# First transform stage of an FFT convolution: one 121-column product, or two column tiles of 64 and 57

## The chip, the cores and the metric

The kernel runs on one core of one Trainium2 chip. The metric is the device time of one execution in microseconds. The kernel before takes 2770.51 us, the median of 2 runs (2769.9 to 2771.11).

## What is computed

The reference chains three things. First a long convolution with a gate: with `u = x * v` of shape (2, 12480, 128) and a filter made by a small two-layer network, `y = irfft(rfft(u) * rfft(h))` along the sequence, and the result is `x * y`. Then two pairs of dense layers follow on the 24960 tokens: `(g @ w_out)` with `h = tokens @ w_in`, once with `g = h * cos(h)` and once with `g = h * clip(h + 3, 0, 6) / 6`, width 128 to 2048 to 128.

```python
Uf = np.fft.rfft(u, n=L, axis=1)
Hf = np.fft.rfft(h_filt, n=L, axis=0)
y = np.fft.irfft(Uf * Hf[None, :, :], n=L, axis=1)[:, :S, :]
return (x * y)
```

The change touches the convolution alone.

## The kernel before, in words

The convolution is done as a two-dimensional transform: a series of 111 x 113 points (N1 x N2) is transformed along the 111 first, then along the 113. It runs in 64 iterations (`for i in range(NG)`), each on two of the 128 channels, with the stages of several iterations interleaved by hand: the program is written in the order in which each engine is to run it, and every engine works through its own queue in that order.

The names that matter are these.

- `uf` (made on DVE, line 225) and `hf` (made on POOL, line 237) hold, for each series, 57 columns of sums at columns 0 to 56 and 57 columns of differences at columns 64 to 120 (OD = 64, KE = 121). Columns 57 to 63 are zero.
- `f1` is the constant table of the transform along 111 points: 56 cosines and 56 negative sines in 112 columns (K1 = 56).
- `s1(i, g)` is the first transform stage, three times per iteration: g = 2 for the filter, g = 0 and 1 for the two batch entries. It makes four products (line 252). Each has 121 columns of `uf` or `hf` as the stationary operand and the 112 columns of `f1` as the moving operand, and puts 121 partitions x 112 values into the PSUM tile `ap`. The operands are float32, and the trace shows each such product as two passes, a weight load and a matmul each, so four products are eight passes.
- ACT then copies `ap` to the SBUF tile `at`, in two instructions: partitions 0 to 63 with the cosine half first (line 254), and partitions 64 to 120 with the two halves exchanged (line 255).
- `s2h` and `s2u` (line 364) are the second stage, on `at`: PSUM tiles `xh` and `xp`. `s2i` (line 408, PSUM tile `bp`) and `s1i` (line 422, PSUM tile `v`) transform back. DVE and POOL do the element-wise work between them; `fin` on POOL (lines 450 to 464) finishes a result, and `make_q` and `make_hf` on POOL (lines 204 to 237) prepare the next input. Two `decoder` generators unpack the weights of the dense layers in the same loop, on DVE, ACT and POOL.

On TensorE's queue an iteration reads: four products of `s1` for the filter, four of `s2i`, four of `s1`, four of `s2i`, four of `s1`, then `s2h`, `s2u` and `s1i`. The dense layers come after the loop and make up most of the time.

Of the kernel before, what the change touches and what calls it, by code (L numbers as in the profile page):

```python
# [9 lines left out]
FP32 = mybir.dt.float32  # L10
# [13 lines left out]
N1, N2 = 111, 113  # L24
N = N1 * N2
NP1 = 112
K1 = 56
M2 = 57
MP = 2 * M2
OD = 64  # L30
KE = OD + M2
# [12 lines left out]
def kernel(  # L44
# [19 lines left out]
    nc = tc.nc  # L64
# [84 lines left out]
    def conv_phase(cctx):  # L149
        const = cctx.enter_context(tc.tile_pool(name="const", bufs=1))  # L150
# [8 lines left out]
            k = sum(d >= o for o in HS[1:])  # L159
            return h_p[k][:, d - HS[k]:d - HS[k] + n, :]  # L160

        f1 = const.tile([N1, 2 * K1], FP32, name="f1")
        f2 = const.tile([N2, MP], FP32, name="f2")
        sig = const.tile([NP1, MP], FP32, name="sig")
        cs = const.tile([KE, 2, N2], FP32, name="cs")
# [2 lines left out]
        uf = [const.tile([N1, B, 2, CH, 128], FP32, name=f"uf{k}") for k in range(2)]  # L168
        hf = [const.tile([N1, 2, CH, 128], FP32, name=f"hf{k}") for k in range(2)]
# [72 lines left out]
        def s1(i, g, pool=None):  # L242
            if i >= NG:
                return
            if i not in a_t:
                a_t[i] = p_2.tile([KE, 2, 12, K1], FP32, tag="at", name="at")
            at = a_t[i]
            ap = (pool or ps_a).tile([KE, 4, 2, K1], FP32, tag="a", name="ap")
            for q in range(4):
                s, c = divmod(q, CH)  # L250
                st = (uf[i % 2][:, g, s, c] if g < 2 else hf[i % 2][:, s, c])[:, :KE]
                nc.tensor.matmul(out=ap[:, q].rearrange("p z k -> p (z k)"), lhsT=st, rhs=f1)  # L252
            src = ap.rearrange("p q z k -> p z q k")
            nc.scalar.copy(at[:OD, :, 4 * g:4 * g + 4, :], src[:OD])
            nc.scalar.copy(at[OD:, ::-1, 4 * g:4 * g + 4, :], src[OD:])

        with ExitStack() as hctx:
            hp = hctx.enter_context(tc.tile_pool(name="hp", bufs=1))
# [69 lines left out]
            for k in range(len(chunks)):  # L328
                if k + 8 < len(chunks):
                    load_pos(k + 8)  # L330
                if k + 1 < len(chunks):
                    mlp(k + 1)
                filt(k)
                if k == len(chunks) - 3:
                    make_p(0, ps_r)
                    make_u(0)
                if k >= len(chunks) - 2:
                    s1(0, k - len(chunks) + 2)
                if k == 3:
                    nc.sync.dma_start(out=sig, in_=c_sig)  # L340
                    load(0)
                    nc.sync.dma_start(out=f1, in_=c_f1)
                    nc.sync.dma_start(out=cs, in_=c_cs)
                if k == 5:
                    make_q(0)
                    load(1)
                    nc.sync.dma_start(out=f2, in_=c_f2)
                    nc.sync.dma_start(out=gm, in_=c_g)
                if k == 7:
                    make_q(1)  # L350
                if k == 9:
                    load(2)
# [121 lines left out]

        make_hf(0)
        s1(0, 2)
        make_p(1)
        make_u(1)
        make_hf(1)
        for i in range(NG):  # L480
            load(i + 3)
            store(i - 4)
            s1(i + 1, 2)
            s2i(i - 2, 0)
            s1(i + 1, 0, ps_c)
            s2i(i - 2, 1)
            s1(i + 1, 1)
            make_p(i + 2)
            make_q(i + 2)
            make_hf(i + 2)  # L490
            s2h(i)
            if i >= 3:
                mk_w(i - 3)
            step_decode()
            make_u(i + 2)
            if i >= 3:
                fin(i - 3)
            s2u(i)
            if i >= 2:
                s1i(i - 2)  # L500
            mk_pq(i)
            mk_y(i)
# [236 lines left out]
    with tc.manual_schedule():  # L739
        nc.gpsimd.memset(b_exp, 1150.0)  # L740
        nc.gpsimd.memset(b_max, 254.0 * 2.0 ** 23)
        nc.gpsimd.memset(b_one, 1.0)
        with ExitStack() as cctx:
            conv_phase(cctx)
        with ExitStack() as mctx:
            moe_phase(mctx)


def _order():
    ord2 = np.concatenate([np.arange(1, M2), [0], N2 - np.arange(1, M2)])  # L750
    return ord2, (N2 * np.arange(N1)[:, None] + N1 * ord2[None, :]) % N
# [15 lines left out]
def _constants():  # L767
    ord2, idx = _order()
    n1 = np.arange(N1)
    f32 = np.float32  # L770
    k1 = np.arange(K1)
    th1 = 2 * np.pi * ((n1[:, None] * k1[None, :]) % N1) / N1
    f1 = np.concatenate([np.cos(th1), -np.sin(th1)], axis=1)
    k2 = np.arange(N2)
    thi = 2 * np.pi * ((k2[:, None] * ord2[None, :M2]) % N2) / N2
    f2 = np.concatenate([np.cos(thi), np.sin(thi)], axis=1)
    cs = np.zeros((KE, 2, N2))
    cs[:M2, 0] = cs[:M2, 1] = np.cos(thi.T)
    cs[OD:, 0], cs[OD:, 1] = np.sin(thi.T), -np.sin(thi.T)
    wt = (np.where(k1 == 0, 1.0, 2.0) * 0.5 / N)[:, None]  # L780
    co, si = np.cos(th1.T) * wt, np.sin(th1.T) * wt
    g = np.zeros((2 * K1, 2, NP1))
    g[:K1, 0, :N1], g[K1:, 0, :N1] = co, -si
    g[:K1, 1, :N1], g[K1:, 1, :N1] = -si, -co
    win = np.zeros((N1, MP))
    win[:, :N2] = np.where(idx < S, np.exp(f32(-0.01) * idx.astype(f32)), 0.0)
    sig = np.zeros((NP1, MP))
    sig[:N1, :N2] = 1.0 - 2.0 * (idx % 2)
    return idx, [a.astype(f32) for a in (f1, cs, f2, g, win, sig)]
# [53 lines left out]
```

## Time and profile before

| What | Value |
|---|---|
| median of the runs | 2770.51 us (2769.9 to 2771.11) |
| the profiled execution's own time | 2773.05 us |
| its span | 2771.3 us |
| loop of the convolution | about 40 to 553 us of the span |
| dense layers | from about 572 us to the end |
| TensorE busy over the span | 2740.0 us (99%) |
| granted TensorE clock, mean | 0.995 of 2.4 GHz |

An engine's busy time is the union of its instructions' times. The end of a matmul is modelled, and one matmul's record overlaps the next one's; what a pass costs in a stream is therefore the distance from one start to the next and not the recorded duration. Weight loads (PEld) run beside the matmuls (PE).

### The profile page before, as it was taken

What the parts mean: (1) busy time and instruction counts of PE and PEld (TensorE: products, weight loads), DVE (VectorE), ACT (ScalarE), POOL (GpSimd) and SP (SyncE); (2) the same over time, 40 slices, a digit from 0 to 9 for tenths busy, and PEclk for the clock granted to TensorE, in tenths of its full rate; (3) what the DMA queues carried; (4) which work ended last, traced back from release to release, by engine and by line L of the source; (5) the groups of instructions that cost most, each with busy time, mean ns of one, the idle gap of its engine ahead of it and who ended that gap; (6) DMA issues with size and microseconds to landing.
All of it is one profiled execution on the core that took longest, in us unless ns stands there. A gap on an engine that the chain in (4) does not pass through costs nothing.

```text
span 2771.3 us, 39495 instructions
## 1 busy us (share of the span) xinstructions
PE 2740.0 (99%) x12941; PEld 2205.5 (80%) x12941; DVE 2348.6 (85%) x3182; ACT 2268.1 (82%) x3287; POOL 2448.3 (88%) x1551
## 2 busy tenths in 40 slices
PE   8999999979999999999999999999999999999999
PEld 7777777768888888888888888888888888888888
DVE  6888888778888888888888888888888888888887
ACT  4777777778888888888888888888888888888885
POOL 5899999878989888889888898988889888889897
PEclk9999999989999999999999999999999999999999
DMA  3333333210000000000000000000000000000000
GB/s 113 87 95 96 94 96 87 72 31 8 16 9 16 8 16 8 16 8 16 12 13 16 8 16 8 16 8 16 8 16 16 8 16 8 16 8 16 8 8 12
DMA packets 88289, 79.50 MB, mean 29 GB/s; under 512 B 57139, under 2 KB 78870, under 8 KB 88086
## 3 DMA queue, kind: packets, MB, share of 16 engines
q1 hardware_dynamic: 87798, 76.77, 10.0%
q8 instruction: 106, 1.74, 0.3%
q14 instruction: 97, 0.79, 0.1%
q10 hardware_dynamic: 288, 0.20, 0.0%
HBM read 51.19 MB, written 25.74 MB: 28 GB/s over the span
## 4 chain that ended last, share of the span: by engine, by line
PE 88%; POOL 9%; ACT 1%; DVE 1%; issue 1%; DMA 0%; POOLq 0%; SPq 0%; ACTq 0%; DVEq 0%
PE acc L676 39%; PE hb L610 20%; PE ha L610 19%; PE ap L252 3%; PE bp L408 2%; PE xp L364 2%; PE v L422 2%; POOL z L464 2%; POOL hf L237 1%; POOL z L463 1%; POOL z L450 1%; POOL q L204 1%; PE xh L364 1%; POOL q L207 1%; POOL hm L232 1%
## 5 line engine op out<-in xcount | busy, mean ns | idle before, releaser
L666 POOL TENSOR_TENSOR lo<-g,hi 128x1024 fp32r<-128x1024 f32 (+1 forms) x390 | 939.4, 2409 | 239.9 <-PE ha L610 160.6
L641 POOL TENSOR_TENSOR lo<-g,hi 128x1024 fp32r<-128x1024 f32 (+1 forms) x392 | 941.9, 2403 | 8.4 <-ACT hi L638 7.8
L620 ACT ACTIVATE k<-ha,biasq 128x512 int32<-128x512 f32 (+1 forms) x768 | 507.8, 688 | 310.2 <-PE ha L610 305.8
L631 DVE TENSOR_TENSOR g<-ha,r 128x512 f32<-128x512 f32 (+1 forms) x768 | 500.0, 690 | 286.3 <-ACT r L630 286.2
L610 PE MATMUL ha<-xh,wi 128*128 128x512 f32 (+1 forms) x1536 | 546.1, 396 | 10.5 <-ACT xh L587 7.4
L610 PE MATMUL hb<-x2h,vi 128*128 128x512 f32 (+1 forms) x1564 | 554.7, 395 | 0.3 <-DVE g L631 0.3
L630 ACT ACTIVATE r<-r,biaspi 128x512 f32<-128x512 f32 (+1 forms) x776 | 520.6, 720 | 0.2
L621 DVE SCALAR_TENSOR_TENSOR r<-k,ha 128x512 f32<-128x512 int32 (+1 forms) x768 | 489.8, 679 | 4.0 <-ACT k L620 3.5
L649 DVE SCALAR_TENSOR_TENSOR g<-q,hb 128x1024 f32<-128x1024 f32 (+1 forms) x391 | 473.1, 1210 | 8.8 <-ACT q L648 8.8
L663 DVE SCALAR_TENSOR_TENSOR hi<-q,hb 128x1024 fp32r<-128x1024 f32 (+1 forms) x390 | 470.4, 1206 | 0.0
L648 ACT ACTIVATE q<-hb,bias 128x1024 f32<-128x1024 f32 (+1 forms) x391 | 434.6, 1111 | 21.8 <-PE hb L610 17.9
L676 PE MATMUL acc<-hi,wo 128*128 128x512 f32 (+1 forms) x1568 | 429.4, 396 | 0.0
L676 PE MATMUL acc<-hi,vo 128*128 128x512 f32 (+1 forms) x1568 | 427.6, 395 | 0.0
L638 ACT CAST hi<-g 128x1024 fp32r<-128x1024 f32 (+1 forms) x388 | 403.0, 1039 | 0.0
L610 PEld LDWEIGHTS ha<-xh,wi 128*128 128x128 f32 x1536 | 289.9, 189 | 78.8 <-issue 11.5
L676 PEld LDWEIGHTS acc<-hi,wo 128*128 128x128 f32 x1568 | 295.8, 189 | 69.2
L610 PEld LDWEIGHTS hb<-x2h,vi 128*128 128x128 f32 x1564 | 294.6, 188 | 70.0 <-ACT k L620 0.7
L676 PEld LDWEIGHTS acc<-hi,vo 128*128 128x128 f32 x1568 | 294.6, 188 | 65.9
L610 PE MATMUL hb<-x2l,vi 128*128 128x512 f32 (+1 forms) x782 | 308.1, 394 | 0.0
L610 PE MATMUL ha<-xl,wi 128*128 128x512 f32 (+1 forms) x768 | 303.2, 395 | 0.0
L676 PE MATMUL acc<-lo,wo 128*128 128x512 f32 (+1 forms) x784 | 246.5, 396 | 0.0
L676 PE MATMUL acc<-lo,vo 128*128 128x512 f32 (+1 forms) x784 | 245.8, 394 | 0.0
(116 smaller groups left out, 3408.2 us busy)
## 6 DMA issues: line engine op xcount, KB each, us to landing
x<-in_x_dram SPq DMA_DIRECT2D x64, 199.5 KB
v<-in_v_dram SPq DMA_DIRECT2D x64, 199.5 KB
scr<-z SPq DMA_DIRECT2D x128, 98.9 KB
out_dram<-o SPq DMA_DIRECT2D x47, 256.0 KB
xf<-scr SPq DMA_DIRECT2D x17, 256.0 KB
wst<-in_wi_dram SPq DMA_DIRECT2D x8, 512.0 KB
wst<-in_wo_dram SPq DMA_DIRECT2D x8, 512.0 KB
pt<-in_post_dram SPq DMA_DIRECT2D x14, 224.0 KB
```

The lines of the kernel that those rows point to most:

```text
L610: nc.tensor.matmul(out=hs[c][:, 0, :n], lhsT=w["i", e][:, sl], rhs=r[:, :n], start=(k == 0), stop=(k == 2))
L620: nc.scalar.activation(out=k[:, c, :n], in_=h, func=ACTF.Identity, bias=biasq, scale=1.0 / TWO_PI)
L621: nc.vector.scalar_tensor_tensor(out=un.r[:, c, :n], in0=k[:, c, :n], scalar=-TWO_PI, in1=h, op0=ALU.mult, op1=ALU.add)
L630: nc.scalar.activation(out=rc, in_=rc, func=ACTF.Sin, bias=biaspi, scale=1.0)
L631: nc.vector.tensor_tensor(out=un.g[:, c, :n], in0=h, in1=rc, op=ALU.mult)
L638: nc.scalar.copy(un.hi[:, :, :n], un.g[:, :, :n])
L641: nc.gpsimd.tensor_tensor(out=un.lo[:, :, :n], in0=un.g[:, :, :n], in1=un.hi[:, :, :n], op=ALU.subtract)
L648: nc.scalar.activation(out=un.r[:, c, :n], in_=h, func=ACTF.Relu, bias=bias3, scale=1.0)
L649: nc.vector.scalar_tensor_tensor(out=un.g[:, c, :n], in0=un.r[:, c, :n], scalar=6.0, in1=h, op0=ALU.min, op1=ALU.mult)
L663: nc.vector.scalar_tensor_tensor(out=un.hi[:, c, :n], in0=un.r[:, c, :n], scalar=6.0, in1=h, op0=ALU.min, op1=ALU.mult)
L666: nc.gpsimd.tensor_tensor(out=un.lo[:, :, :n], in0=un.g[:, :, :n], in1=un.hi[:, :, :n], op=ALU.subtract)
L676: nc.tensor.matmul(out=acc[e][:, :n], lhsT=w["o", e][:, sl], rhs=r[:, c, :n], start=(u == 0 and c == 0 and k == 0), stop=(u == KFF // 2 - ...
```

## The change

The four products of `s1` are made in two pieces each. One takes the 64 columns of the sums and writes PSUM partitions 0 to 63; the other takes the 57 columns of the differences and writes PSUM partitions 64 to 120. In the compiled program the first has a tile of 128 rows x 64 columns of the array at column 0, the second one of the same size at column 64; every other product of the kernel has the whole 128 x 128 array. The table `f1` gets a third block, the cosines again, so that the second piece can use columns 56 to 167 (negative sines first, then cosines): the halves come out exchanged already, and one ACT instruction copies all 121 partitions.

```diff
-        f1 = const.tile([N1, 2 * K1], FP32, name="f1")
+        f1 = const.tile([N1, 3 * K1], FP32, name="f1")
...
-                st = (uf[i % 2][:, g, s, c] if g < 2 else hf[i % 2][:, s, c])[:, :KE]
-                nc.tensor.matmul(out=ap[:, q].rearrange("p z k -> p (z k)"), lhsT=st, rhs=f1)
-            src = ap.rearrange("p q z k -> p z q k")
-            nc.scalar.copy(at[:OD, :, 4 * g:4 * g + 4, :], src[:OD])
-            nc.scalar.copy(at[OD:, ::-1, 4 * g:4 * g + 4, :], src[OD:])
+                st = uf[i % 2][:, g, s, c] if g < 2 else hf[i % 2][:, s, c]
+                o = ap[:, q].rearrange("p z k -> p (z k)")
+                nc.tensor.matmul(out=o[:OD], lhsT=st[:, :OD], rhs=f1[:, :2 * K1])
+                nc.tensor.matmul(out=o[OD:], lhsT=st[:, OD:KE], rhs=f1[:, K1:])
+            nc.scalar.copy(at[:, :, 4 * g:4 * g + 4, :], ap.rearrange("p q z k -> p z q k"))
...
-    f1 = np.concatenate([np.cos(th1), -np.sin(th1)], axis=1)
+    f1 = np.concatenate([np.cos(th1), -np.sin(th1), np.cos(th1)], axis=1)
```

TensorE's queue for one iteration of the loop reads as follows in the kernel before (x4: four instructions of that form; L252 is `s1`, L408 is `s2i`, L364 is `s2h` and `s2u`, L422 is `s1i`):

```order
L252 MATMUL ap<-f_79,hf_86 121x112 x4
L408 MATMUL bp<-f_80,y 112x114 x4
L252 MATMUL ap<-f_79,uf_84 121x112 x4
L408 MATMUL bp<-f_80,y 112x114 x4
L252 MATMUL ap<-f_79,uf_84 121x112 x4
L364 MATMUL xh<-at,cs 113x224 x2
L364 MATMUL xp<-at,cs 113x448 x2
L422 MATMUL v<-b,gm 112x456 x2
```

The first of the three `s1` groups of an iteration, and what follows it, in the changed kernel:

```order
L253 MATMUL ap<-f_79,hf_86 64x112
L254 MATMUL ap<-f_79,hf_86 57x112
L253 MATMUL ap<-f_79,hf_86 64x112
L254 MATMUL ap<-f_79,hf_86 57x112
L253 MATMUL ap<-f_79,hf_86 64x112
L254 MATMUL ap<-f_79,hf_86 57x112
L253 MATMUL ap<-f_79,hf_86 64x112
L254 MATMUL ap<-f_79,hf_86 57x112
L408 MATMUL bp<-f_80,y 112x114 x4
```

The groups stay where they were; each has eight instructions in place of four, alternating between the two column tiles. Each float32 instruction is two passes again, so a group has sixteen passes in place of eight. Six times in an iteration the queue goes from column tiles to the whole array or back.

ACT's queue, one iteration, before:

```order
L254 COPY at<-ap 64x2x224
L255 COPY at<-ap 57x2x224
L409 COPY b<-bp 112x456
L254 COPY at<-ap 64x2x224
L255 COPY at<-ap 57x2x224
L409 COPY b<-bp 112x456
L254 COPY at<-ap 64x2x224
L255 COPY at<-ap 57x2x224
L215 COPY p<-x 111x2x114
L370 COPY hs<-xh 113x448
L423 COPY v2s<-v 112x456
```

and in the changed kernel:

```order
L255 COPY at<-ap 121x2x224
L409 COPY b<-bp 112x456
L255 COPY at<-ap 121x2x224
L409 COPY b<-bp 112x456
L255 COPY at<-ap 121x2x224
L215 COPY p<-x 111x2x114
L370 COPY hs<-xh 113x448
L423 COPY v2s<-v 112x456
```

Three copies are gone from each iteration; nothing else moved on ACT.

## Rows read from the trace of the kernel before

**Rows 1.** The page: span, and each engine's busy us, share of the span, instructions.
```profile
span 2771.3 us, 39495 instructions
PE 2740.0 (99%) x12941; PEld 2205.5 (80%) x12941; DVE 2348.6 (85%) x3182; ACT 2268.1 (82%) x3287; POOL 2448.3 (88%) x1551
```

**Rows 2.** Busy time by stretch: the loop, its even middle, the dense layers.
```profile
core 0: us, PE busy (x) PEld busy (x) DVE busy (x) ACT busy (x) POOL busy (x), PEclk, DMA share, GB/s
40.00:553.00 513.00, 505.25 (x3273) 396.90 (x3274) 422.12 (x697) 386.39 (x758) 477.26 (x659) 0.99 0.32 89
60.00:540.00 480.00, 475.96 (x3113) 372.97 (x3112) 404.84 (x664) 368.20 (x722) 455.44 (x618) 1.00 0.33 91
...
600.00:2700.00 2100.00, 2096.64 (x8998) 1693.92 (x8997) 1813.23 (x2300) 1791.48 (x2396) 1865.07 (x800) 1.00 0.04 12
```

**Rows 3.** Chain of waits in order of time: start us, us, what; one piece per iteration.
```profile
68.72 1.56 PE v L422 x4
76.65 1.56 PE v L422 x4
84.57 1.56 PE v L422 x4
```

**Rows 4.** Waits, 60 to 540 us: engine line, releaser, total us, times, longest.
```profile
PE ap L252 <- POOL hf L237: 4.0, 4, 1.0
...
PE xh L364 <- ACT at L255: 0.3, 1, 0.3
```

**Rows 5.** Timeline of PE, part of an iteration: start us, us, instructions merged (xcount).
```profile
301.97 1.01 PE L252 MATMUL ap<-f,uf 111*121 111x112 f32 x8
302.81 0.95 PE L408 MATMUL bp<-f,y 113*112 113x114 f32 x8
303.60 1.01 PE L252 MATMUL ap<-f,uf 111*121 111x112 f32 x8
304.45 0.92 PE L364 MATMUL xh<-at,cs 121*113 121x224 f32 x4
305.21 1.67 PE L364 MATMUL xp<-at,cs 121*113 121x448 f32 x4
306.71 0.55 PE L422 MATMUL v<-b,gm 112*112 112x456 f32 x1
```

**Rows 6.** Timeline of the weight loads (PEld) in the same stretch.
```profile
301.87 0.93 PEld L252 LDWEIGHTS ap<-f,uf 111*121 111x121 f32 x8
302.72 0.87 PEld L408 LDWEIGHTS bp<-f,y 113*112 113x112 f32 x8
303.50 0.93 PEld L252 LDWEIGHTS ap<-f,uf 111*121 111x121 f32 x8
...
305.58 0.18 PEld L364 LDWEIGHTS xp<-at,cs 121*113 121x113 f32 x1 [0.20 <-issue]
305.96 0.18 PEld L364 LDWEIGHTS xp<-at,cs 121*113 121x113 f32 x1 [0.20 <-issue]
306.34 0.18 PEld L422 LDWEIGHTS v<-b,gm 112*112 112x112 f32 x1 [0.20 <-issue]
```

**Rows 7.** Tile `ap`: count, duration ns min/median/max, first and last start us.
```profile
L252 PEld LDWEIGHTS ap<-f,uf x1024: 181/186/329, 40.2 to 548.1; 111*121 111x121 f32 x171
L252 PE MATMUL ap<-f,uf x1024: 267/269/545, 40.2 to 548.2; 111*121 111x112 f32 x171
...
L252 PE MATMUL ap<-f,hf x512: 258/269/541, 45.3 to 544.9; 111*121 111x112 f32 x171
L254 ACT COPY at<-ap x192: 522/525/528, 42.0 to 548.5; 64x448 f32<-64x448 f32 x192
L255 ACT COPY at<-ap x192: 527/527/531, 42.6 to 549.0; 57x448 f32<-57x448 f32 x192
```

**Rows 8.** Timeline, first pass after TensorE stood idle: its load and its matmul.
```profile
309.42 0.18 PEld L252 LDWEIGHTS ap<-f,hf 111*121 111x121 f32 x1 [1.75 <-POOL hf L237]
309.42 0.36 PE L252 MATMUL ap<-f,hf 111*121 111x112 f32 x1 [0.99 <-POOL hf L237]
```

## The prediction, made before the changed kernel ran

> **What bounds the kernel now.** I read busy time by engine first. TensorE is busy for 2740 of 2771.3 us [rows 1], so the first question is whether the stage that changes is TensorE's too. The busy time by stretch says so: in the even middle of the loop, 60 to 540 us, TensorE is busy for 475.96 of 480 us, POOL for 455.44, ACT for 368.20 [rows 2]. The reader is to see two things there: TensorE has 4 us to spare in 480, and POOL stands just behind it. The dense layers, 600 to 2700 us, are TensorE's at 2096.64 of 2100 [rows 2], and nothing in them changes.
>
> A busy engine might still wait inside its records, so I looked at the chain of waits and at the waits themselves. In the loop the chain carries one piece of the same `v` products each iteration, at 68.72, 76.65 and 84.57 us: an iteration is 7.93 us [rows 3]. Of TensorE's waits in 60 to 540 us, 4.0 us are for POOL's `hf` and 0.3 us for ACT's copy to `at` [rows 4]. That is the whole idle time. So every microsecond that TensorE's queue gets longer in the loop is paid in full, less these 4 us; every microsecond that ACT saves is worth at most 0.3 us.
>
> Last I read the timeline for what a pass costs in the stream. Eight passes of `ap` take 302.81 - 301.97 = 0.84 us, 0.105 each; eight of `bp` 303.60 - 302.81 = 0.79 us, 0.099 each [rows 5]. The `ap` pass streams fewer columns (112 against 114) and is slower, so it isn't paced by its columns. Its loads are 0.85 / 8 = 0.106 us apart (302.72 - 301.87), those of `bp` 0.098 [rows 6]: with 121 columns against 112 the `ap` pass is paced by its weight load, at 0.106 / 121 = 0.88 ns a column. What the streaming alone would take I get from `xh` and `xp`: 224 columns at 0.76 / 4 = 0.190 us, 448 at 1.50 / 4 = 0.375 us [rows 5], so 0.83 ns a column and 0.005 us besides; 112 columns make 0.098 us. An `ap` product, two passes, now costs 0.211 us.
>
> **The change, part by part.** *ACT.* 192 copies of 0.525 us go [rows 7], about 101 us of ACT, and the remaining copy has the same 448 elements per partition as the 0.527 us one. I cost the gain at 0.3 us, that is at nothing: ACT is busy for 77% of the middle of the loop and TensorE hardly waits for it [rows 2, 4]. If ACT did bind somewhere, less work there could only help, and POOL caps that: the loop cannot run faster than POOL's 455.44 in 480, so the most that anything can win here is 24.6 / 480 x 513 = 26 us, under 1%.
>
> *The table `f1`* grows by 56 columns and is loaded once, before the loop; I cost it at nothing, covered by the filter stage before 40 us.
>
> *TensorE, the passes.* 768 products become 1536 instructions, 3072 passes in place of 1024 + 512 = 1536 [rows 7]. The two tiles lie in different columns of the array and write different partitions, so passes of one may run beside passes of the other. If they do, two things remain per product. Streaming: two passes per tile side by side, 2 x 0.098 = 0.196 us. Loading: (64 + 57) columns twice at 0.88 ns, 0.212 us, if loads follow one another. I take the larger, since that is what paces this stage today: 0.001 us more than now, x 768 = +1 us. The lower end is 0.196 us, -0.015 x 768 = -11 us. The upper end is that nothing runs side by side: 4 x 0.098 = 0.392 us, +0.181 x 768 = +139 us.
>
> *TensorE, the change of shape.* The groups of column-tile passes stand between whole-array ones, and the new queue goes 372 times from one division of the array to the other (six per iteration, fewer at the ends of the loop). No row of before shows such a change. The nearest row from below is a change of stage within one division: from `ap` to `bp` and back the starts keep their pitch [rows 5], so 0 us. Less than 0 is excluded, since nothing is left out at the change. From above: a pass is recorded for 269 ns [rows 7] and its successor starts after 105, so it is in the array for another 0.164 us; if the array must be empty before it is divided anew, the change costs that. The next load cannot then lie beside a running pass either. What an uncovered load costs is seen after an idle stretch: the first pass lasts 0.36 us in place of 0.269 [rows 8], 0.09 us more. Together 0.254 us. With the whole recorded load of 0.186 us [rows 7] in place of 0.09 it would be 0.35 us.
>
> I take 0.254 us. The rows show overlap of consecutive passes only within one division; a pass of the new one sends its sums down columns that the old one still uses, and an emptied array is just the state of [rows 8]. 372 x 0.254 = +94.5 us; the ends are 0, 61 (0.164) and 130 us (0.35).
>
> Here a rule stands beside the rows. The rows show no price at all between stages [rows 5]. The Trainium skill, "TensorEngine Tiling (Array Packing)", section "Key Properties", says that a change of tiling mode, not of tile alone, drains TensorE. By the unbroken pitch of the rows the sum would be 2772 us; by the rule, priced with the rows as above, 2862 us. No run here shows the rule yet.
>
> *Sum.* +1 + 94.5 - 4 (TensorE's idle time, which a later TensorE no longer has, since POOL's work per iteration stays at 455.44 / 480 x 7.93 = 7.5 us) = +91.5 us. Against the profiled execution's 2773.05 us that is 2864.5; the median of the runs is 2.5 us lower, so 2862 us. An iteration becomes 7.93 + 6 x 0.254 = 9.45 us.
>
> **The rivals.** About 2% (55 us) is what a measurement of this kernel can tell from no change: below 2715 is faster, above 2826 slower.
>
> *A, the forecast:* tiles side by side, the array emptied at each change of shape. 2862 us; its own range by the prices above, 2828 to 2898. Chance 0.30.
>
> *B, not slower:* tiles side by side, and the change of shape costs what any change of stage costs today. For it: the unbroken pitch [rows 5]. Against: those passes all share one division. 2770.5 + 1 = 2772 us, down to 2760 if loads into different tiles also run side by side. It decides below (55 - 1 + 4) / 372 = 0.156 us per change. Chance 0.29.
>
> *C, the change doesn't do what it says:* the passes run one after another. For it: no two starts in the rows are closer than one pass of that size takes alone [rows 5]. +139 - 4: 2905 us, chance 0.11; with the 94.5 us besides, 3000 us, chance 0.08.
>
> *D, loads only one step ahead:* each load starts when the pass before it has started, never earlier, as those of `xp` and `v` do: 305.58, 305.96, 306.34, one per pass [rows 6]. With alternating tiles the first pass of a tile then waits for a load that could begin only when the other tile's second pass began: 64 x 0.88 = 0.056 and 57 x 0.88 = 0.050 us. Per product 2 x 0.098 + 0.056 + 0.050 = 0.302 us, +0.091 x 768 = +70, less 4: 2836 us, chance 0.07; with the price of the changes 2931 us, chance 0.05.
>
> *E, no load is hidden:* a load waits for the passes under way, in either tile. 0.392 + 0.212 = 0.604 us per product, +0.393 x 768 = +302: 3069 us, chance 0.09. Against it stands that every load of `ap` lies beside a pass today [rows 5, 6]. The Trainium skill, "TensorE: Matmul & The Clock Gate", section "The mechanism" of Part 3, says that loads overlap with matmuls under way only when their row groups differ, and both tiles here use the same rows; the trace of before disagrees, for the whole array at least.
>
> **How the numbers follow.** Faster by over 2% would take more than POOL allows: 0.01. Within 2%: B, and 0.03 of A for a price under 0.156 us: 0.32. Slower: the rest, 0.67. The predicted time is A's. The range reaches from B's low end, 2760, to 2935, which takes in A, B, D with and without the changes, and C alone; left out are C with the changes, E and a true gain, 0.18.
>
> **What will show it.** In the changed trace: 1536 + 1536 passes of the two pieces; the distance from the first start of an `s1` group to the first start of the `s2i` group behind it, now 0.84 us. A: about 0.85 us within the group, and a hole of about 0.25 us at both its edges, with the first load behind it uncovered. B: no holes. C: sixteen starts 0.098 us apart, 1.57 us a group. D: 1.2 us a group, starts in an uneven beat. E: 2.4 us. In all of them ACT's busy time falls by 101 us and POOL's waits grow; the dense layers keep their time. I am wrong in kind if POOL or ACT, not TensorE, ends the waits in the loop, or if the dense layers move.

## The result, and the profile after

The changed kernel takes 2809.75 us (2809.0 to 2810.5, 2 runs) against 2770.51 before: the ratio is 1.014, with a 95% interval of 1.0123 to 1.0156. That is 39 us slower. The forecast was 92 us slower. The time lies within the range, it lies below what the forecast case allowed for itself (2828 to 2898), and it lies inside the 2% to which I had given 0.32.

The first lines of the page after, span and busy time by engine, answer to [rows 1]:

```profile
span 2808.7 us, 42188 instructions
PE 2780.8 (99%) x14477; PEld 2187.1 (78%) x14477; DVE 2345.4 (84%) x3182; ACT 2172.7 (77%) x3095; POOL 2439.4 (87%) x1551
```

The span grew by 37.4 us. TensorE has 1536 more passes (14477 against 12941) and is busy for 40.8 us longer; ACT has lost 95 us. By stretch, as [rows 2] (PE, PEld, DVE, ACT, POOL busy, then the granted clock):

```profile
60.00:540.00 480.00, 480.00 (x4217) 336.04 (x4217) 374.06 (x616) 261.00 (x507) 419.90 (x579) 1.00 0.33 86
```

TensorE now has no counted idle time in the middle of the loop, POOL has gone from 455 to 420 of 480 us and ACT from 368 to 261: everything but TensorE has become slack. The chain of waits in order of time, as [rows 3], has only TensorE in it there:

```profile
308.85 1.56 PE v L422 x4
310.41 0.91 PE ap L253 x8
311.32 0.97 PE bp L408 x8
312.29 0.91 PE ap L253 x8
313.20 0.97 PE bp L408 x8
314.17 0.91 PE ap L253 x8
315.08 0.94 PE xh L364 x4
316.02 1.50 PE xp L364 x4
317.53 1.55 PE v L422 x4
```

From `v` to `v` an iteration is 8.68 us (317.53 - 308.85), against 7.93.

The timeline of TensorE shows why. Start and duration in us; the last two pairs of a first-stage group, the `s2i` group behind it, and the first pairs of the next group:

```profile
302.29 0.26 PE L253 MATMUL ap<-f,hf 111*64 111x112 f32 x1
302.29 0.26 PE L254 MATMUL ap<-f,hf 111*57 111x112 f32 x1
302.38 0.26 PE L253 MATMUL ap<-f,hf 111*64 111x112 f32 x1
302.38 0.26 PE L254 MATMUL ap<-f,hf 111*57 111x112 f32 x1
302.57 1.04 PE L408 MATMUL bp<-f,y 113*112 113x114 f32 x8
303.54 0.31 PE L253 MATMUL ap<-f,uf 111*64 111x112 f32 x1
303.55 0.30 PE L254 MATMUL ap<-f,uf 111*57 111x112 f32 x1
303.69 0.26 PE L253 MATMUL ap<-f,uf 111*64 111x112 f32 x1
303.69 0.26 PE L254 MATMUL ap<-f,uf 111*57 111x112 f32 x1
```

Three things are to be seen. The passes of the two tiles start together, and a pair follows a pair after 0.096 us (302.29, 302.38): the tiles do run side by side, and a pair costs less than the one pass of 0.105 us that it replaces [rows 5]. From the last pair to the first `bp` pass there are 0.19 us (302.38 to 302.57) where a pair takes 0.096, so about 0.093 us are lost; I call this the hop. And `bp`'s eight passes now take 302.57 to 303.54 = 0.97 us, where 0.79 were enough before: one hop of 0.093 us at the end of it, back into the tiles, and 0.09 us at its start. The rest of the group, from its second pass on, shows that start:

```profile
302.76 0.85 PE L408 MATMUL bp<-f,y 113*112 113x114 f32 x7
```

The second `bp` pass comes 0.19 us after the first and not 0.098: the first pass's weight load did not lie beside a running pass, as in [rows 8]. The row of that load shows it:

```profile
302.57 0.37 PEld L408 LDWEIGHTS bp<-f,y 113*112 113x112 f32 x3
```

It starts with its own pass at 302.57, where the first `bp` load of the kernel before starts 0.09 us ahead of its pass (302.72 in [rows 6], 302.81 in [rows 5]). Into the tiles the same happens on a smaller scale: 303.54 to 303.69 is 0.15 us, 0.05 more than a pair, as the first pair's durations are 0.05 longer.

So one change of division costs about 0.093 + 0.05 = 0.145 us into the tiles and 0.093 + 0.09 = 0.183 us out of them, 0.164 on average. The chain gives the same from whole groups: (0.97 - 0.79 + 0.91 - 8 x 0.096) / 2 = 0.16. The bill: 372 x 0.164 = +61 us for the changes; 1536 x (0.096 - 0.1055) = -15 us for pairs of passes in place of single ones; about -5 us for TensorE's waits on POOL, which are gone (e5, which takes them out of the kernel before, is 4.8 us faster). That makes +41 us, and +39 were measured.

The weight loads of the two tiles, in the same place:

```profile
303.54 0.13 PEld L253 LDWEIGHTS ap<-f,uf 111*64 111x64 f32 x1
303.55 0.13 PEld L254 LDWEIGHTS ap<-f,uf 111*57 111x57 f32 x1
303.60 0.14 PEld L253 LDWEIGHTS ap<-f,uf 111*64 111x64 f32 x1
303.60 0.13 PEld L254 LDWEIGHTS ap<-f,uf 111*57 111x57 f32 x1
303.69 0.14 PEld L253 LDWEIGHTS ap<-f,uf 111*64 111x64 f32 x1
303.69 0.13 PEld L254 LDWEIGHTS ap<-f,uf 111*57 111x57 f32 x1
```

They too run side by side, one tile's beside the other's.

### The profile page after: what moved, and what is told of

Read it like the earlier page. It is cut to its first block, busy times and chain, and to the rows that moved or that the text cites. A ratio compares the mean times of both kernels' runs of the same rounds, so it can differ in the third digit from the quotient of the medians.

```text
span 2808.7 us, 42188 instructions
## 1 busy us (share of the span) xinstructions
PE 2780.8 (99%) x14477; PEld 2187.1 (78%) x14477; DVE 2345.4 (84%) x3182; ACT 2172.7 (77%) x3095; POOL 2439.4 (87%) x1551
## 4 chain that ended last, share of the span: by engine, by line
PE 97%; ACT 1%; DVE 1%; issue 0%; DMA 0%; SPq 0%; POOL 0%; ACTq 0%; DVEq 0%
PE acc L676 38%; PE hb L610 19%; PE ha L610 19%; PE ap L253 6%; PE bp L408 4%; PE v L422 3%; PE xp L364 3%; PE xh L364 2%; PE hps L308 1%; PE rp L292 0%; ACT k L620 0%; ACT r L630 0%; PE ap L254 0%; ACT hi L638 0%; DVE g L631 0%
## 5 line engine op out<-in xcount | busy, mean ns | idle before, releaser
L610 PE MATMUL ha<-xh,wi 128*128 128x512 f32 (+1 forms) x1536 | 545.0, 395 | 13.2 <-ACT xh L587 7.4
```

Source lines behind the costliest of these rows:

```text
L610: nc.tensor.matmul(out=hs[c][:, 0, :n], lhsT=w["i", e][:, sl], rhs=r[:, :n], start=(k == 0), stop=(k == 2))
```

## The experiments

The theory to be tested: TensorE's queue sets the loop; each change between column tiles and the whole array costs about 0.164 us; the tiles themselves save 15 us, because a first-stage pass was paced by its weight load; the copy on ACT is worth nothing. The rivals: the cost goes with the number of passes; the loss belongs to the first stage's tiles as such; the single copy wins something that hides a larger loss. Beside each time stands that of the kernel before, measured with it.

### e1: the tiles, with two copies

```diff
-            nc.scalar.copy(at[:, :, 4 * g:4 * g + 4, :], ap.rearrange("p q z k -> p z q k"))
+            src = ap.rearrange("p q z k -> p z q k")
+            nc.scalar.copy(at[:OD, :, 4 * g:4 * g + 4, :], src[:OD])
+            nc.scalar.copy(at[OD:, :, 4 * g:4 * g + 4, :], src[OD:])
```

> The changed kernel, but the results are copied by two ACT instructions again (partitions 0 to 63, then 64 to 120), so only the tiling is left of the change. Theory (TensorE's queue sets the loop; the time is lost at the changes between column tiles and whole array): ACT's 192 copies more, 0.53 us each, 101 us in all, lie beside TensorE's work; 2810 us, within 3 us of the changed kernel. Rival (the single copy wins something that hides a larger loss on TensorE): 2820 us or more.

Measured: 2811.47 us, before 2771.37, ratio 1.0146 (1.0132 to 1.0159). Against before it is +40.1 us, where the changed kernel is +39.2: the merged copy is worth about 1 us at most, and nothing in the loop, where e1 too takes 8.68 us from `v` to `v` (301.17 to 309.85 in its chain of waits). The busy time by stretch:

```profile
60.00:540.00 480.00, 480.00 (x4222) 336.16 (x4217) 374.52 (x617) 345.84 (x672) 418.50 (x578) 1.00 0.33 87
```

ACT works 85 us more in these 480 than in the changed kernel (345.84 against 261.00), and TensorE is busy for all 480 us in both.

### e2: the second group of the queue in tiles as well

```diff
-                nc.tensor.matmul(out=src[:, q, :], lhsT=y_t[i][:, 4 * g + q, :], rhs=f2)
+                for a, e in ((0, 64), (64, 2 * K1)):
+                    nc.tensor.matmul(out=src[a:e, q, :], lhsT=y_t[i][:, 4 * g + q, a:e], rhs=f2)
```

> The changed kernel, with the products of s2i (line 408) also in two column tiles (64 and 48). The order stays; the groups s1, s2i, s1, s2i, s1 of an iteration now share one division of the array, so 132 changes of division are left of 372. Theory: a change costs 0.164 us on average (0.145 into the tiles, 0.183 out of them), so 240 fewer give -39 us: 2771 us, a little more if POOL starts to bind. Rival (the cost lies in the number of passes: 39 us over 1536 added ones, 0.025 us each): 1024 more passes, +26 us, 2836 us.

Measured: 2770.31 us, before 2771.37, ratio 0.9996 (0.9987 to 1.0004). With 240 changes fewer and 1024 passes more, the whole loss is gone. The rival by passes is refuted; against e1 the difference is 41 us, 0.17 us for each change that is gone (a little of it is the single copy and faster `bp` passes). The timeline of TensorE, from the last pair of a first-stage group over a `bp` group to the next pair:

```profile
306.45 0.26 PE L253 MATMUL ap<-f,hf 111*64 111x112 f32 x1
306.45 0.26 PE L254 MATMUL ap<-f,hf 111*57 111x112 f32 x1
306.54 0.95 PE L409 MATMUL bp<-f,y 113*64 113x114 f32 x16
307.32 0.26 PE L253 MATMUL ap<-f,uf 111*64 111x112 f32 x1
```

There is no hole: 0.09 us into the `bp` group, and 0.78 us for its sixteen passes, a little less than its eight took before. The first `bp` load is hidden again, 0.09 us ahead of its pass and beside the last `ap` pair:

```profile
306.45 0.33 PEld L409 LDWEIGHTS bp<-f,y 113*64 113x64 f32 x6
```

### e4: only the second group in tiles

The same edit of `s2i`, made in the kernel before; the first stage keeps its whole array and its two copies.

> The kernel before, with s2i alone in two column tiles (64 and 48); the first stage is untouched. 248 changes of division. Theory: 248 x about 0.165 = +41 us, less 4 us of idle time and 2 us for passes of 0.096 in place of 0.098 us: 2806 us. Rival (cost by passes): 1024 added ones at 0.025 us, 2796 us. Second rival (the loss belongs to the first stage's tiles, to its results that are read later, or to its copy): no change, 2771 us.

Measured: 2803.91 us, before 2771.37, ratio 1.0117 (1.0103 to 1.0131): +32.5 us with 248 changes, where +35 were expected. The loss comes without any tile in the first stage, so it belongs to the changes and not to that stage, its results or its copy. The rival by passes had 2796, nearer to the result than the rival by stage, but e2 had refuted it already. Timeline:

```profile
303.11 0.99 PE L409 MATMUL bp<-f,y 113*64 113x114 f32 x16
304.03 1.10 PE L252 MATMUL ap<-f,uf 111*121 111x112 f32 x8
305.06 0.99 PE L409 MATMUL bp<-f,y 113*64 113x114 f32 x16
```

The `ap` group, whole array now between two tile groups, takes 1.03 us from start to start where it took 0.84 [rows 5]; the `bp` group takes 0.92 where it took 0.79. These are the two prices again, the other way round: 0.84 + 0.183 = 1.02, and 0.78 + 0.145 = 0.93.

### e3: every product of the loop in tiles

The edit of e2, and the same cut at 64 in `s2h`, `s2u` and `s1i`:

```diff
-                nc.tensor.matmul(out=o[z], lhsT=cs[:, z, :], rhs=a[:, z, q0:q1, :])
+                for p, e in ((0, 64), (64, N2)):
+                    nc.tensor.matmul(out=o[z][p:e], lhsT=cs[:, z, p:e], rhs=a[:, z, q0:q1, :])
...
-                nc.tensor.matmul(out=v[z][:, r], lhsT=gm[:, z, :], rhs=b[:, r, z * M2:(z + 1) * M2])
+                for p, e in ((0, 64), (64, NP1)):
+                    nc.tensor.matmul(out=v[z][p:e, r], lhsT=gm[:, z, p:e], rhs=b[:, r, z * M2:(z + 1) * M2])
```

> As the run before, and the products of s2h, s2u and s1i (lines 364, 422) in two column tiles as well: 4 changes of division are left in the program. Theory: -368 x 0.164 = -60 us against the changed kernel, 2750 us; below the kernel before by what the first stage saves (0.096 in place of 0.105 us per pass, 15 us) and by a little idle time; POOL, at 7.5 us an iteration, may hold it up to 2760. Rival (cost by passes, 0.025 us each): +45 us, 2855 us.

Measured: 2766.87 us, before 2771.37, ratio 0.9984 (0.9975 to 0.9993). The direction is the theory's, but the time is 17 us above its 2750, and 7 above the 2760 to which I had thought POOL might hold it. Busy time by stretch:

```profile
60.00:540.00 480.00, 477.80 (x6278) 382.58 (x6276) 406.73 (x666) 279.61 (x547) 458.21 (x622) 1.00 0.35 91
```

Three of its waits (engine line, releaser, total us, times, longest):

```profile
DVE uf L225 <- POOL q L207: 25.0, 26, 1.5
PEld ap L253 <- POOL hf L237: 16.0, 25, 1.2
PE ap L253 <- POOL hf L237: 2.2, 6, 0.4
```

POOL is busy for 458 of 480 us, and both DVE's `uf` and TensorE's `hf` loads now wait for it. TensorE's 477.80 look full all the same: of the 16.0 us that the loads wait, only 2.2 us count as idle time of the passes, since a wait that is shorter than the recorded tail of the pass before isn't counted. Whether POOL is the whole reason had to be tested.

### e5 and e6: one POOL instruction moved to DVE

```diff
 def make_q(i):
-            nc.gpsimd.tensor_tensor(out=q[:, :, 1], in0=q[:, :, 0], in1=sg(1), op=ALU.mult)
 def make_u(i):
             nc.vector.tensor_tensor(out=p[:, :, 1], in0=p[:, :, 0], in1=sg(0), op=ALU.mult)
+            nc.vector.tensor_tensor(out=q[:, :, 1], in0=q[:, :, 0], in1=sg(1), op=ALU.mult)
```

The control, on the kernel before:

> The kernel before, with one POOL instruction per iteration (the product of q with the signs, line 207, 0.7 us) moved to DVE, in make_u. A control for the next two runs. TensorE's queue is unchanged, so only its waits on POOL, 4 to 5 us in the loop, can go: 2767 us, 2764 to 2771.

Measured: 2766.45 us, before 2771.24, ratio 0.9979 (0.997 to 0.9988). And on e3:

> All products of the loop in column tiles, as e3, and the POOL instruction moved to DVE. Theory (e3 stayed 17 us above its expected 2750 because POOL, at 458 of 480 us, took over as the bound): with POOL relieved TensorE's shorter queue shows, 2752 us, 2748 to 2756. Rival (the missing time lies on TensorE itself: passes in tiles are slower in the second and later stages, or the two tiles drift apart): 2763 to 2767, no more below e3 than e5 is below the kernel before.

Measured: 2752.04 us, before 2771.24, ratio 0.993 (0.9917 to 0.9943). It is 14 us below the control, about the 15 us that the tiles save on the passes; in e3 POOL had hidden them. Of the versions that leave nothing out this is the fastest: it beats the kernel before by 19 us (0.7%), of which the move alone is worth 5 (e5), and the changed one by 58. Busy time by stretch, of e5:

```profile
60.00:540.00 480.00, 479.41 (x3144) 377.12 (x3143) 450.82 (x731) 372.47 (x730) 417.41 (x567) 1.00 0.34 91
```

and of e6:

```profile
60.00:540.00 480.00, 479.52 (x6456) 347.80 (x6452) 465.98 (x739) 286.75 (x559) 423.73 (x572) 1.00 0.35 93
```

In e6 POOL has fallen from 458 to 424 us and TensorE sets the pace again; DVE, at 466, is the next in line.

### e7: fewer stationary columns instead of tiles

```diff
-KE = OD + M2
+KE = 112
...
-    cs[OD:, 0], cs[OD:, 1] = np.sin(thi.T), -np.sin(thi.T)
+    cs[OD:, 0], cs[OD:, 1] = np.sin(thi.T)[:KE - OD], -np.sin(thi.T)[:KE - OD]
```

made in the kernel of e5. It leaves the last 9 of the 57 columns of differences out of the transform, so what it computes is no longer the convolution.

> The kernel of e5 (whole array, POOL relieved) with 112 stationary columns in the first stage in place of 121: the last 9 columns of the differences are left out of the transform. Nothing is tiled. Theory (a first-stage pass is paced by its weight load, 0.88 ns a column, and the tiles win because the loads of two tiles run at once): a pass falls from 0.105 to 0.098 us, 1536 x 0.0075 = 11 us below e5: 2756 us. Rival (the pass is paced by something else that the tiles shorten): as e5, 2767 us.

Measured: 2754.77 us, before 2771.24, ratio 0.9937 (0.9923 to 0.9951): 11.7 us below e5, where 11 were expected. Timeline of TensorE:

```profile
303.37 0.95 PE L408 MATMUL bp<-f,y 113*112 113x114 f32 x8
304.16 0.95 PE L252 MATMUL ap<-f,uf 111*112 111x112 f32 x8
304.95 0.95 PE L408 MATMUL bp<-f,y 113*112 113x114 f32 x8
306.52 0.93 PE L364 MATMUL xh<-at,cs 112*113 112x224 f32 x4
307.28 1.67 PE L364 MATMUL xp<-at,cs 112*113 112x448 f32 x4
```

An `ap` group takes 0.79 us in place of 0.84, with the same 112 columns streamed. The second stage sums over 112 rows in place of 121 here, but that gains nothing: from `xh` to `xp` it is 0.76 us (306.52 to 307.28), as in [rows 5]. So the load of nine stationary columns more than 112 paced the first stage. That the tiles save the same thing is argued from it: their loads run side by side, and a pair is at the pace of the columns streamed.

## Why the prediction was right and wrong

- **The bound.** Right. The profile had shown TensorE with 4 us to spare in 480; the lengthening of its queue was paid in full, and it now waits for nobody there.
- **ACT costed at nothing.** Right to about 1 us: e1, which gives ACT its copies back, adds 40.1 us to the kernel before where the changed kernel adds 39.2.
- **The passes, +1 us: wrong, -15.** I had let the loads of the two tiles follow one another, 0.212 us a product. They run side by side, and the streaming of 0.096 us per pair is left. I had that case as the lower end, -11. e7 shows by another way that the load was the pace.
- **The change of shape, 0.254 us: the mechanism right, the size wrong; this is the step that failed.** e2, e4 and e1 show a loss that follows the number of changes: 372 give +40, 248 give +32, with 132 the changes and the passes' gain cancel. But the hop, the prediction's time for emptying the array, was 0.093 us and not 0.164. I had read it from the recorded duration less the pitch, which takes the modelled end of a matmul for the time until the array is free; the next division's first pass started 0.19 us after the last pair, while that pair's record runs for 0.26. The uncovered load added 0.09 us out of the tiles, as I had read it from [rows 8], and 0.05 into them, where 64 columns are loaded and not 112. No record shows the array itself empty; that the hop is the emptying is an inference, and what speaks for it is that the hop is the same behind passes of 112, 114 and 456 columns and absent where the division stays. My end of 0.164 for the whole of it happens to be the measured mean, for other reasons than I gave.
- **The sum.** 372 x 0.090 us too much for the changes makes 33 us, the passes 16 us. Without these two errors the forecast would have been +42.
- **The rivals.** B had the tiles right and the free change wrong; its point of decision, 0.156 us, lies close to the measured price, and the result fell on its side of the 2% because the passes gained. C, D and E are refuted by the timeline: pairs start together, 0.096 us apart, with their loads covered.
- **The rules of the Trainium skill.** The Trainium skill, "TensorEngine Tiling (Array Packing)", "Key Properties", has a change of tiling mode drain TensorE. The trace agrees, with a hole of 0.093 us at every change, and e2 shows none between stages of one division. The Trainium skill, "TensorE: Matmul & The Clock Gate", "The mechanism" in Part 3, has one line by which loads overlap with matmuls under way only where row groups differ, beside a sentence that also lets a load run ahead when it goes to a background weight buffer. The trace disagrees with the line as it stands, since the loads at 303.60 and 303.69 us lie beside passes of both tiles, and both tiles use the same rows; it doesn't tell whether such a buffer is the reason.

Open: the first `xh` load comes 3.0 us earlier in the changed kernel (at 50.4 us against 53.4). Of these, 1.6 us are there at the first `ap` load (38.6 against 40.2), before anything that the change touches, and stay unexplained. From that load to `xh` it takes 11.8 us in the changed kernel, 12.9 in e1 (38.3 to 51.2) and 13.2 before: ahead of the loop, where TensorE does wait for others, the single copy seems to win the 1 us by which e1 lies above the changed kernel. The dense layers' share of the span moves by 1 to 2 us between these kernels, also unexplained. These are of the size of the 2 us by which the bill misses the measurement.

## What to carry to other kernels

In this kernel two column tiles ran side by side, with their weight loads beside them, but each change of the division of the array cost 0.164 us on average: count how often the queue changes it, and either tile the neighbours as well or leave the stage whole. Read what a pass costs from starts, and never take the recorded end of a matmul for the moment at which the next may begin. Before a gain on the bounding engine is expected in full, look at the second engine: with POOL at 455 of 480 us the version with all but four changes of division gone won 4 us, and 19 once one POOL instruction had been moved away, 5 of them by the move itself.

## What the runs showed of the hardware that was not expected

- The two tiles need not stay in step. In e3, when `hf` is late, the first tile starts ahead and the second follows 0.35 us later (the annotation is what ended TensorE's idle time):

```profile
303.66 0.41 PE L253 MATMUL ap<-f,hf 111*64 111x112 f32 x2 [0.36 <-POOL hf L237]
304.01 0.30 PE L254 MATMUL ap<-f,hf 111*57 111x112 f32 x1
304.01 0.31 PE L253 MATMUL ap<-f,hf 111*64 111x112 f32 x1
304.15 0.26 PE L254 MATMUL ap<-f,hf 111*57 111x112 f32 x1
...
304.94 0.26 PE L254 MATMUL ap<-f,hf 111*57 111x112 f32 x1
304.95 0.26 PE L410 MATMUL bp<-f,y 113*64 113x114 f32 x1
305.03 0.26 PE L254 MATMUL ap<-f,hf 111*57 111x112 f32 x1
```

  The second tile stays two passes behind, so the first tile starts on the `bp` group (304.95) before the second has started its last `ap` pass (305.03), which stands ahead of `bp` in the program. Across tiles, passes need not start in the order of the queue.
- The hop does not grow with the size of the pass before it. Behind a `v` pass of 456 columns, in the changed kernel:

```profile
301.18 0.55 PE L422 MATMUL v<-b,gm 112*112 112x456 f32 x1
301.66 0.31 PE L253 MATMUL ap<-f,hf 111*64 111x112 f32 x1
```

The first tile pass starts 0.48 us after it, where `v` passes follow one another after 0.39 (1.56 / 4 in the chain): 0.09 us again.
